# One step of a fused attention and mixing kernel: the low rank term's second product in one pass on stacked strips, and products of ones where the plan has TensorE wait

## The chip, the cores and the metric

The kernel runs on one core of a Trainium2 chip. The metric is the device time of one execution in microseconds (us), the median of several runs. TensorE (PE) multiplies into PSUM, VectorE (DVE) and ScalarE (ACT) empty PSUM and do the elementwise work, GpSimd (POOL) does elementwise work in SBUF, and SyncE (SP) issues most transfers, in order.

## What is computed

Three stages follow one another for a batch of 4, 576 positions and 512 features; the change touches the second line of the middle one.

```python
# 1. windowed attention, 8 heads of 64, window 128, with a linear bias
scores = where(mask, q @ k.T / 8 + bias, -1e9); x = softmax(scores) @ v      # (4, 576, 512)
# 2. low rank mixing over positions, then a two layer product
h = (x.transpose(0, 2, 1) @ U) @ V         # U is 576 x 32, V is 32 x 576
u = x + h.transpose(0, 2, 1)               # the low rank term is added to x
x = u + maximum(u @ w_ch1, 0) @ w_ch2      # 512 -> 2048 -> 512
# 3. gated mixing
a = maximum(x @ w_in, 0); g, v = a[..., :512], a[..., 512:]
v = (v - mean(v)) / sqrt(var(v) + 1e-6)
out = (g * (einsum('ts,bsd->btd', w_spatial, v) + b_spatial)) @ w_out
```

## The kernel before

All work is held in a list of tasks, each with an engine (or a choice of engines), a cost in planned microseconds, and the buffers that it reads and writes. `Plan.run` schedules the list eight times (`forward`, and `latest` for new priorities), takes the plan that ends first, and emits the instructions of the tasks in that order. Each engine then works its own instructions strictly in the emitted order. A task may sit on ACT or DVE (`copy` with two engines) or on POOL or DVE, as the plan finds better. The costs in the list are the planner's alone; what an instruction takes is seen in the trace.

The attention of a batch goes through four pairs of heads (`heads`): scores on TensorE (L1044), the bias and maximum on DVE (L1055), the exponential on ACT (L1060), the division on DVE or POOL (L1082, L1080; in the first batch it is put off to L1135), transpositions on TensorE (L1090) with copies to SBUF (L416 on ACT, L417 on DVE), and the product with v (L1128). The result is `u`, one tile of 128 features by 576 positions for each pair of heads. `turned` transposes it (L1155). `low_rank` then works in two steps:

- `mix` (L1171) multiplies with U. The four pairs' results, 32 rows each, lie as four strips in one PSUM tile `t`; a copy takes them to `th` in SBUF (tile th, L416).
- `up` (L1184) multiplies each strip with the matching 32 rows of V, for 288 positions at a time, in float32. The four pairs use four strips of rows of the array at once. DVE adds each product to `u` (L1189).

In the first batch `low_rank` is called twice, for pairs 0 and 1 and for pairs 2 and 3; in the other three once for all pairs. Float32 products show as two records each in the trace, products in float32r as one. Elsewhere the kernel gets float32's accuracy from float32r by splitting an operand into a high part (rounded) and a low part (the rest), with three products.

The low rank weights come early: V arrives as raw 64 bit words (raw), is put together on ACT and DVE into `v4` (L452 to L465, tile v), and four transfers (L983) spread it to `v32`.

When `u` of a batch is complete, ACT and POOL split it (L529, L532) and TensorE begins a group of the two layer product for 512 positions (`early_group`: L545 to L547, evacuated by L551 and L552; then L584 to L586, added by L594). Three such groups are worked among the attention of later batches. Their weights are put together on DVE (L458 to L465, tile st), too. The last low rank term is worked at 184 us; after it TensorE goes on through the two layer product and the gated stage until the end. `turn_over` (L991) is a task of before: nine float32 products of ones (tile hot) at the very beginning.

## Time and profile before

| | us |
|---|---|
| median of three runs (714.07 to 714.25) | 714.19 |
| the profiled execution | 713.79 |
| its span, from the first to the last instruction | 712.0 |

The profiled execution has 1.79 us outside its span, and it lies 0.40 us under the median. Busy time counts an engine's instructions from start to modelled end; matmuls overlap, so that a start to start distance says more than a duration. "Idle before" is the time in which the engine had nothing in hand, with what ended it.

### The profile page before, as it was taken

The page shows a single profiled execution, that of the slowest core. Times are in us where ns is not written, and L with a number is a line of the kernel's source. Part 1 is how long each engine was busy: PE and PEld are TensorE (multiplying, and loading weights), DVE is VectorE, ACT ScalarE, POOL GpSimd, SP SyncE. Part 2 cuts the span into 40 slices and gives each one's busy share as a digit, 9 for nine tenths or more (in the row PEclk, how much of TensorE's full clock was granted, in tenths as well). Part 3 has the DMA queues.
Part 4 walks back from the last instruction along what each step waited for, and adds up shares of the span by engine and source line. Part 5 has one row for each costly group of instructions (what it writes and reads, how often), then busy time and mean ns, then how long its engine had stood idle before and what let it go on. Part 6 is the DMA issues. An engine that isn't in the chain of part 4 may idle for free.

```text
span 712.0 us, 14829 instructions
## 1 busy us (share of the span) xinstructions
PE 701.7 (99%) x5434; PEld 637.8 (90%) x5434; DVE 576.0 (81%) x1637; ACT 394.0 (55%) x1082; POOL 75.0 (11%) x114
## 2 busy tenths in 40 slices
PE   8989999999999999999999999999999999999998
PEld 6767778778799999999999999999998898898896
DVE  6999996775597999999695998696589989859561
ACT  7878666564353655547253562544267566566352
POOL 2243330310400000000000000040010100100000
DMA  8865212210074166628475555447694202100102
GB/s 233 280 221 161 66 52 82 72 53 2 1 225 157 42 228 220 223 106 267 149 225 175 168 195 185 144 148 264 239 386 174 80 30 68 54 22 0 60 1 75
DMA packets 58799, 98.48 MB, mean 138 GB/s; under 512 B 8357, under 2 KB 38309, under 8 KB 58726
## 3 DMA queue, kind: packets, MB, share of 16 engines
q1 hardware_dynamic: 58437, 97.23, 41.2%
q8 instruction: 43, 0.70, 0.4%
q14 instruction: 31, 0.25, 0.1%
q10 hardware_dynamic: 288, 0.30, 0.1%
HBM read 67.67 MB, written 29.54 MB: 137 GB/s over the span
## 4 chain that ended last, share of the span: by engine, by line
PE 88%; DVE 7%; ACT 2%; DMA 1%; issue 1%; POOL 0%; SPq 0%; POOLq 0%; ACTq 0%
PE sc L586 8%; PE sc L584 8%; PE sc L585 8%; PE at L885 6%; PE at L886 6%; PE at L887 6%; PE at L1128 3%; PE sc L1044 2%; PE sc L1423 2%; PE sc L1421 2%; PE sc L1422 2%; PE at L1090 2%; PE at L1423 2%; PE at L1421 2%; PE at L1422 2%; PE acc L584 2%
## 5 line engine op out<-in xcount | busy, mean ns | idle before, releaser
L584 PE MATMUL sc<-h,wa 128*128 128x384 f32 (+1 forms) x328 | 110.6, 337 | 0.0
L585 PE MATMUL sc<-h,wa 128*128 128x384 f32 (+1 forms) x328 | 110.5, 337 | 0.0
L586 PE MATMUL sc<-hl,wa 128*128 128x384 f32 x320 | 108.7, 340 | 0.0
L1060 ACT ACTIVATE p<-p,nmax 128x192 f32<-128x192 f32 (+2 forms) x144 | 61.5, 431 | 10.2 <-DVE nmax L1055 10.0
L584 PEld LDWEIGHTS sc<-h,wa 128*128 128x128 f32 x328 | 61.6, 188 | 0.3
L585 PEld LDWEIGHTS sc<-h,wa 128*128 128x128 f32 x328 | 61.5, 187 | 0.3
L933 DVE TENSOR_TENSOR y<-sc,y 128x384 f32<-128x384 f32 (+1 forms) x96 | 40.7, 450 | 25.6 <-PE sc L586 25.3
L885 PE MATMUL at<-xd,wa 128*128 128x384 f32 x180 | 60.9, 338 | 0.0
L886 PE MATMUL at<-xd,wa 128*128 128x384 f32 x180 | 60.8, 338 | 0.0
L887 PE MATMUL at<-xd,wa 128*128 128x384 f32 x180 | 60.8, 338 | 0.0
L586 PEld LDWEIGHTS sc<-hl,wa 128*128 128x128 f32 x320 | 60.1, 188 | 0.0
L1055 DVE CUSTOM_DVE_ANT_0 p<-sc,bias 128x192 f32<-128x192 f32 (+2 forms) x144 | 40.3, 328 | 12.7 <-PE sc L1044 12.4
L905 ACT COPY c<-at 128x384 f32<-128x384 f32 x54 | 25.8, 478 | 39.2 <-PE at L887 38.9
L416 ACT CAST wa<-st 128x256 fp32r<-128x256 f32 (+1 forms) x62 | 28.1, 475 | 25.2 <-DVE st L465 13.1
L897 ACT ACTIVATE h<-c 128x384 fp32r<-128x384 f32 x54 | 28.4, 526 | 19.7 <-DVE c L892 19.5
L892 DVE TENSOR_TENSOR c<-at,c 128x384 f32<-128x384 f32 x54 | 29.8, 551 | 8.2 <-PE at L887 4.9
L885 PEld LDWEIGHTS at<-xd,wa 128*128 128x128 f32 x180 | 33.8, 188 | 0.0
L886 PEld LDWEIGHTS at<-xd,wa 128*128 128x128 f32 x180 | 33.8, 188 | 0.0
L887 PEld LDWEIGHTS at<-xd,wa 128*128 128x128 f32 x180 | 33.8, 188 | 0.0
L1044 PE MATMUL sc<-kr,qr 64*64 64x192 f32 (+2 forms) x576 | 31.7, 319 | 1.2 <-DMA qr<-in_qT 0.7
L1090 PE MATMUL at<-ident,p 128*128 128x128 f32 x208 | 31.1, 281 | 1.5 <-DVE p L1082 1.4
L1090 PEld LDWEIGHTS at<-ident,p 128*128 128x128 f32 x208 | 23.0, 140 | 10.4 <-issue 3.3
(407 smaller groups left out, 2007.7 us busy)
## 6 DMA issues: line engine op xcount, KB each, us to landing
wa<-in_w SPq DMA_DIRECT2D x32, 512.0 KB, 4.3
xd<-formsa SPq DMA_DIRECT2D x24, 192.0 KB, 3.0
qr<-in_qT SPq DMA_DIRECT2D x15, 288.0 KB, 3.3
kr<-in_kT SPq DMA_DIRECT2D x15, 288.0 KB, 4.0
vr<-in_v SPq DMA_DIRECT2D x16, 256.0 KB, 4.3
raw<-in_w_in SPq DMA_DIRECT2D x8, 512.0 KB, 3.9
kepts<-raw SPq DMA_DIRECT2D x14, 288.0 KB, 2.1
out<-h SPq DMA_DIRECT2D x15, 256.0 KB, 2.0
```

Source lines behind the costliest of these rows:

```text
L584: nc.tensor.matmul(o, wt[:, 0, 0, c], hh[:, j], start=i == 0 and x == 0, stop=False, skip_group_check=True)
L585: nc.tensor.matmul(o, wt[:, 1, 0, c], hh[:, j], start=False, stop=False, skip_group_check=True)
L586: nc.tensor.matmul(o, wt[:, 0, 0, c], hl[:, j], start=False, stop=i == len(wts) - 1, skip_group_check=True)
L885: nc.tensor.matmul(o.ap(), wh()[:, k], xh.ap(), start=start and k == 0, stop=False, skip_group_check=True)
L886: nc.tensor.matmul(o.ap(), wl()[:, k], xh.ap(), start=False, stop=False, skip_group_check=True)
L887: nc.tensor.matmul(o.ap(), wh()[:, k], xl.ap(), start=False, stop=k == 1, skip_group_check=True)
L892: P.add("DVE", dve(N3), lambda: nc.vector.tensor_tensor(out=out.ap(), in0=ps_.ap(), in1=sb.ap(), op=ALU.add), r=[ps_, sb], w=[out], prio=0)
L933: P.add("DVE", dve(m), lambda acc=acc, dst=dst, s=s, m=m, o=o: nc.vector.tensor_tensor(out=dst[:, s : s + m], in0=acc[:, 0, o : o + m], in ...
L1044: nc.tensor.matmul(s[o : o + 64, c0 : c0 + k1 - k0], qr[d, 64 * t : 64 * t + 64], kr[d, k0:k1], start=True, stop=True, skip_group_check=True)
L1055: nc.vector.tensor_tensor_reduce(out=o(), in0=s[:, c0 : c0 + nk], in1=bias_t[:, pair, t % 2, 192 - nk :], scale=-0.125, scalar=BIG, op0=AL ...
L1060: nc.scalar.activation(out=o(), in_=o(), func=AF.Exp, scale=-1.0, bias=nmax[:, sl, t : t + 1], accum_out=sums[:, sl, t : t + 1])
L1090: P.add("PE", 0.109, lambda pt=pt, n_=n_, s0=s0: nc.tensor.transpose(pt[:, n_ - s0], p[:, n_ * 128 : n_ * 128 + 128], ident), r=[p.part(t) ...
```

## The change

`up` no longer takes one strip of 32 rows per product. For each pair the strip of `t` is split into a high and a low part, and three strips are laid into `four`, a tile with 128 rows for each pair (the fourth strip stays zero): the high part once, the low part once, and the high part once more. `v32` now holds the high part of V in its first 64 rows and the low part in the other 64, so that one float32r product over all 128 rows is the sum of three partial products. Each pair's strips take three small instructions: a copy on ACT or DVE, a difference on DVE, and the second copy on ACT or DVE. They are planned at 0.27 us on ACT and 0.3 on DVE, longer than the planner's formula gives a copy of all four strips at once. Every product is a task of its own, with its own PSUM tile. V's split costs a copy on ACT and a difference on DVE ahead of the four transfers.

The other part is `fill`: a task on TensorE may carry a float32 product of ones into the tile that it is about to write. `Plan.run` emits up to three of them ahead of a task that the plan starts before 90 us, one for each 0.25 us that the plan leaves TensorE without work before it. The tasks that carry one are the scores, the transpositions, the spreading of the divisors (L1101), the product with v, `mix`, the new products and the first layer of the early groups.

```diff
@@ -138,10 +138,11 @@
 class Task:
-    __slots__ = ("eng", "cost", "emit", "ways", "prio", "deps", "succ", "left", "before", "start", "lat", "port", "mode")
+    __slots__ = ("eng", "cost", "emit", "ways", "prio", "deps", "succ", "left", "before", "start", "lat", "port", "mode", "fill")
...
 PASSES = 8
+FILL = 0.25, 3, 90.0
@@ -156,12 +157,12 @@
-    def either(self, ways, r=(), w=(), prio=0, lat=0.0, deps=(), port=False, mode=None):
+    def either(self, ways, r=(), w=(), prio=0, lat=0.0, deps=(), port=False, mode=None, fill=None):
...
         t = Task()
-        t.ways, t.prio, t.lat, t.port, t.mode = {way[0]: way for way in ways}, prio, lat, port, mode
+        t.ways, t.prio, t.lat, t.port, t.mode, t.fill = {way[0]: way for way in ways}, prio, lat, port, mode, fill
         d = set(deps)
@@ -220,7 +221,12 @@
             self.latest()
+        end = 0.0
         for t, t.eng, t.cost, t.emit, t.start in min(plans)[2]:
+            if t.eng == "PE":
+                for _ in range(min(FILL[1], int((t.start - end) / FILL[0])) if t.fill and t.start < FILL[2] else 0):
+                    t.fill()
+                end = t.start + t.cost
             t.emit()
@@ -552,6 +558,10 @@
+    def ones_into(o):
+
+        return lambda: nc.tensor.matmul(o(), hot.ap(), hot.ap(), start=True, stop=True, skip_group_check=True)
+
     def early_group(t0, n, wts, prio, evac, spare):
@@ -562,7 +572,8 @@
                 P.add("PE", 12 * mm(n), lambda f1=f1, j=j, wt=wt: first_of(f1[:, j], wt, hs, ls),
-                      r=[p for x in hs + ls for p in x[2]] + [wt.part(0), wt.part(1)], w=[f1], prio=prio)
+                      r=[p for x in hs + ls for p in x[2]] + [wt.part(0), wt.part(1)], w=[f1], prio=prio,
+                      fill=ones_into(lambda f1=f1, j=j: f1[:, j, :128]))
             hh, hl = r_h.new([128, w, n], F32R), r_h.new([128, w, n], F32R)
@@ -965,24 +976,27 @@
                   w=[p.part("zero")], prio=-1)
-    r_xt, r_th = Ring(in_att, "xt", 2), Ring(in_att, "th", 2)
+    r_xt, four = Ring(in_att, "xt", 2), constant("four", [128, 4, 128], F32R)
+    P.add("POOL", 0.3, lambda: nc.gpsimd.memset(f32(four.ap()), 0.0), w=[four.part(pair) for pair in range(4)], prio=-1)
...
     u32 = constant("u32", [128, 5, RANK], F32)
-    v32 = constant("v32", [128, S], F32)
+    v32 = constant("v32", [128, S], F32R)
...
         n = S // 2
-        v4 = constant("v4", [128, 1, n], F32)
+        v4, v4h = constant("v4", [128, 1, n], F32), Ring(in_left, "y", 0, more=["y_4"]).new([128, n], F32R)
         single(v4, [(0, block(V, 0, RANK, i // 2 * n, i // 2 * n + n), slice(RANK * i, RANK * i + RANK)) for i in range(4)],
                1, n, prio_v, None, early_v)
+        P.add("ACT", act(n, 0.09), lambda: nc.scalar.copy(out=v4h.ap(), in_=v4[:, 0]), r=[v4], w=[v4h], prio=K["vc"])
+        minus(("DVE",), n, lambda: v4[:, 0].bitcast(F32R), lambda: v4[:, 0], lambda: f32(v4h.ap()), r=[v4h], w=[v4], prio=K["vc"])
         for q in range(2):
-            for d in range(2):
-                P.dma(64, n, lambda q=q, d=d: nc.sync.dma_start(
-                    out=v32[64 * d : 64 * d + 64, q * n : q * n + n], in_=v4[64 * q : 64 * q + 64, 0]),
-                    r=[v4], w=[v32.part((q, d))], prio=K["vc"])
+            for d, (src, t) in enumerate(((lambda: f32(v4h.ap()), v4h), (lambda: v4[:, 0], v4))):
+                P.dma(64, n, lambda q=q, d=d, src=src: nc.sync.dma_start(
+                    out=f32(v32[64 * d : 64 * d + 64, q * n : q * n + n]), in_=src()[64 * q : 64 * q + 64]),
+                    r=[t], w=[v32.part((q, d))], prio=K["vc"])
@@ -1045,7 +1059,8 @@
             scored = [P.add("PE", 4 * max(sum(64 * min(t + 1, 3) for _, t, _ in tiles if t % 2 == o) for o in range(2)) / 2400 + 0.1,
-                  score, r=[x.part(c) for x in (qr, kr) for c in CUTS if c < 64 * tiles[-1][1] + 64], w=list(s.values()), deps=filled, prio=p0 + 1, mode="quarters")]
+                  score, r=[x.part(c) for x in (qr, kr) for c in CUTS if c < 64 * tiles[-1][1] + 64], w=list(s.values()), deps=filled, prio=p0 + 1, mode="quarters",
+                  fill=ones_into(lambda s=next(iter(s.values())): s[:, :128]))]
             for _, t, _ in tiles:
@@ -1088,7 +1103,7 @@
                     P.add("PE", 0.109, lambda pt=pt, n_=n_, s0=s0: nc.tensor.transpose(
-                        pt[:, n_ - s0], p[:, n_ * 128 : n_ * 128 + 128], ident), r=[p.part(t) for t in ts] + [p.part("zero")], w=[pt], prio=p0 + 5)
+                        pt[:, n_ - s0], p[:, n_ * 128 : n_ * 128 + 128], ident), r=[p.part(t) for t in ts] + [p.part("zero")], w=[pt], prio=p0 + 5, fill=ones_into(lambda pt=pt, n_=n_, s0=s0: pt[:, n_ - s0]))
                 copy(engines("e", "ACT"), 128 * (s1 - s0), lambda s0=s0, s1=s1: x[:, s0:s1], pt.ap, PSUM, r=[pt], w=[x.part(g)], prio=p0 + 6)
@@ -1101,7 +1116,7 @@
-                P.add("PE", 320 * 4 / 2400 + 0.1, spread, r=[dg, ones], w=rs, prio=p0 + 4.5, mode="quarters")
+                P.add("PE", 320 * 4 / 2400 + 0.1, spread, r=[dg, ones], w=rs, prio=p0 + 4.5, mode="quarters", fill=ones_into(lambda: rs[0][:, :2]))
                 r = r_d.new([128, 9, D], F32)
@@ -1129,7 +1144,8 @@
-            P.add("PE", 13 * 64 * 4 / 2400 + 0.2, pv, r=[vr, last] + [x.part(g) for g in range(4)], w=os_, prio=p0 + 8, mode="quarters")
+            P.add("PE", 13 * 64 * 4 / 2400 + 0.2, pv, r=[vr, last] + [x.part(g) for g in range(4)], w=os_, prio=p0 + 8, mode="quarters",
+                  fill=ones_into(lambda: os_[0][:, :2]))
             if plain:
@@ -1154,7 +1170,7 @@
                         x[:, c - c0, i], ub[:, TOK[c][0] : TOK[c][0] + 128], ident),
-                        r=[ub.part(0), ub.part(1)], w=[x], prio=p0 + 8.5)
+                        r=[ub.part(0), ub.part(1)], w=[x], prio=p0 + 8.5, fill=ones_into(lambda x=x, c=c, c0=c0, i=i: x[:, c - c0, i]))
             copy(engines("h", "ACT"), 256 * len(cs), lambda c0=c0, cs=cs: xt[:, c0 : c0 + len(cs)], x.ap, PSUM,
@@ -1162,8 +1178,7 @@
         sc, tp = (r_sc0, r_at0) if b == 0 else (r_sc, r_at)
-        rows = slice(pairs[0] * 32, pairs[-1] * 32 + 32)
-        t, th = tp.new([128, 128], F32), r_th.new([128, 128], F32)
+        t = tp.new([128, 128], F32)
@@ -1172,20 +1187,23 @@
         P.add("PE", 5 * 4 * 128 / 2400 + 0.1, mix, r=[u32] + [xts[h].part(c) for h in {p // 2 for p in pairs} for c in (0, 2, 4)],
-              w=[t], prio=p0, mode="quarters")
-        copy(engines("t", "ACT"), 128, lambda: th[rows], lambda: t[rows], PSUM, r=[t], w=[th], prio=p0 + 0.05)
+              w=[t], prio=p0, mode="quarters", fill=ones_into(t.ap))
+        strip = lambda g: slice(32 * g, 32 * g + 32)
+        for pair in pairs:
+            part, low = four.part(pair), 0 if pair == 1 else 1
+            high = lambda to, pair=pair, **kw: P.either([
+                ("ACT", 0.27, lambda: nc.scalar.copy(out=four[strip(to), pair], in_=t[strip(pair)])),
+                ("DVE", 0.3, lambda: nc.vector.tensor_copy(out=four[strip(to), pair], in_=t[strip(pair)]))], r=[t], w=[part], prio=p0 + 0.05, **kw)
+            high(pair)
+            P.add("DVE", 0.3, lambda pair=pair, low=low: nc.vector.tensor_tensor(
+                out=four[strip(low), pair], in0=t[strip(pair)], in1=f32(four[strip(pair), pair]), op=ALU.subtract), r=[t], w=[part], prio=p0 + 0.05)
+            high(2 if pair < 2 else 0, lat=0.3)
         for s0 in (0, 288):
             sl = slice(s0, s0 + 288)
-            outs = [(sc, tp)[pair % 2].new([128, 288], F32) for pair in pairs]
-
-            def up(sl=sl, outs=outs):
-                for pair, o in zip(pairs, outs):
-                    d = slice(pair * 32, pair * 32 + 32)
-                    nc.tensor.matmul(o.ap(), th[d], v32[d, sl], start=True, stop=True)
-
-            P.add("PE", 4 * 288 / 2400 + 0.1, up, r=[th] + list(v32.parts.values()), w=outs, prio=p0 + 0.1, mode="quarter rows")
-            for pair, o in zip(pairs, outs):
-                ub = u[b][pair]
+            for pair in pairs:
+                o, ub = (sc, tp)[pair % 2].new([128, 288], F32), u[b][pair]
+                P.add("PE", mm(288), lambda pair=pair, o=o, sl=sl: nc.tensor.matmul(o.ap(), four[:, pair], v32[:, sl], start=True, stop=True),
+                      r=[four.part(pair)] + list(v32.parts.values()), w=[o], prio=p0 + 0.1, fill=ones_into(lambda o=o: o[:, :128]))
                 P.add("DVE", dve(288), lambda o=o, ub=ub, sl=sl: nc.vector.tensor_tensor(
```

## Rows read from the trace of the kernel before

**Rows 1.** The page: busy time of the engines, share of the span, instructions

```profile
PE 701.7 (99%) x5434; PEld 637.8 (90%) x5434; DVE 576.0 (81%) x1637; ACT 394.0 (55%) x1082; POOL 75.0 (11%) x114
```

**Rows 2.** Busy time by stretch: stretch, length, engines (instructions), granted clock, DMA

```profile
0.00:20.00 20.00, 17.70 (x296) 13.71 (x296) 12.68 (x70) 15.21 (x63) 4.08 (x17) 1.00 0.81 235
20.00:40.00 20.00, 18.93 (x320) 13.85 (x313) 18.90 (x76) 16.60 (x58) 6.67 (x6) 1.00 0.94 304
40.00:60.00 20.00, 17.80 (x224) 12.70 (x218) 20.00 (x74) 14.55 (x51) 7.05 (x9) 1.00 0.48 154
60.00:80.00 20.00, 19.55 (x253) 15.48 (x248) 20.00 (x71) 17.24 (x56) 10.13 (x15) 1.00 0.44 129
80.00:100.00 20.00, 19.98 (x290) 14.70 (x294) 18.80 (x64) 11.95 (x41) 5.65 (x6) 1.00 0.20 62
```

**Rows 3.** The chain that ended last, by line: 0 to 80 us, then 80 to 190

```profile
by line: DVE p L1055 12.1%; DVE p L1082 11.1%; ACT p L1060 10.6%; DMA qr<-in_qT 8.6%; DVE ph L417 6.4%; DVE st L465 5.3%; PE at L1128 4.6%; DVE st L462 4.6%; issue 4.6%; POOL x L532 3.3%; PE sc L1044 3.2%; DVE st L458 3.1%; DVE h L552 3.0%;
...
by line: PE at L1128 14.8%; PE at L1090 11.8%; PE sc L1044 11.6%; PE acc L584 10.2%; PE acc L586 7.6%; PE acc L585 7.6%; PE f L545 6.9%; PE f L547 6.7%; PE f L546 6.6%; PE at L1155 5.6%; PE sc L1184 3.7%; PE at L1171 3.4%; PE sc L585 1.0%; 
```

**Rows 4.** TensorE in order of time, second batch: start, length, line, records

```profile
88.39 0.40 PE L585 MATMUL acc<-h,wa 128*128 128x512 f32 x1
88.63 0.39 PE L586 MATMUL acc<-h,wa 128*128 128x512 f32 x1
88.94 0.51 PE L1184 MATMUL sc<-v,th 32*128 32x288 f32 x1
...
89.64 0.50 PE L584 MATMUL acc<-h,wa 128*128 128x512 f32 x1
89.98 0.40 PE L585 MATMUL acc<-h,wa 128*128 128x512 f32 x1
```

**Rows 5.** TensorE in order of time, first batch, pairs 0 and 1

```profile
30.50 0.51 PE L1184 MATMUL sc<-v,th 32*128 32x288 f32 x1
...
31.67 0.87 PE L1090 MATMUL at<-ident,p 128*128 128x128 f32 x6
```

**Rows 6.** TensorE in order of time, gated stage: float32r products of 288 columns

```profile
545.18 0.30 PE L1574 MATMUL acc<-wf,x 128*128 128x288 f32 x1
...
545.97 0.29 PE L1577 MATMUL acc<-we,ve 128*128 128x288 f32 x1
```

**Rows 7.** TensorE in order of time, start: the products of ones

```profile
1.04 2.50 PE L991 MATMUL f<-hot 128*128 128x128 f32 x10 [1.04 <-DVE hot L950]
...
4.38 1.16 PE L991 MATMUL f<-hot 128*128 128x128 f32 x8
```

**Rows 8.** Instructions by line or tile: count, shortest, median, longest in ns, starts

```profile
L416 ACT COPY th<-at x5: 260/266/267, 29.1 to 180.9; 128x128 f32<-128x128 f32 x3, 64x128 f32<-64x128 f32 x2
L1189 DVE TENSOR_TENSOR u<-at,u x16: 434/448/453, 31.4 to 185.4; 128x288 f32<-128x288 f32 x16
L602 DVE TENSOR_TENSOR fg<-y,fg x32: 205/215/226, 510.5 to 696.5; 128x64 fp32r<-128x64 f32 x32
```

**Rows 9.** DVE in order of time, from 20 and from 39 us

```profile
20.32 0.82 DVE L1135 TENSOR_TENSOR u<-at,y 128x320 f32<-128x320 f32 x2 [0.49 <-PE at L1128]
...
39.64 3.06 DVE L1082 TENSOR_SCALAR p<-p,rinv 128x192 f32<-128x192 f32 x9
...
42.96 0.45 DVE L1189 TENSOR_TENSOR u<-sc,u 128x288 f32<-128x288 f32 x1
43.32 0.44 DVE L1189 TENSOR_TENSOR u<-at,u 128x288 f32<-128x288 f32 x1
```

**Rows 10.** ACT in order of time, 39 to 46 us

```profile
41.95 0.48 ACT L416 COPY ph<-at 128x384 f32<-128x384 f32 x1 [1.42 <-PE at L1090]
43.60 0.48 ACT L416 COPY ph<-at 128x384 f32<-128x384 f32 x1 [1.17 <-PE at L1090]
```

**Rows 11.** SyncE in order of time, 19 to 24 us: start, length, transfer

```profile
19.86 1.18 SPq L983 DMA_DIRECT2D v<-v  x2
21.14 0.52 SPq L1008 DMA_DIRECT2D qr<-in_qT  x1
```

## The prediction

> **What bounds the kernel now.** I read the page first: TensorE is busy for 701.7 us, 99% of the span [rows 1]. Busy time flatters matmuls, so the second view is the busy time by stretch, where the reader should compare TensorE with DVE: in the first 80 us TensorE has waits of 2.30, 1.07, 2.20 and 0.45 us, 6.0 in all, while DVE is at 18.90 of 20 from 20 us on and at 20.00 of 20 from 40 to 80; from 80 on TensorE is at 19.98 of 20 [rows 2]. The third view, the chain that ended last, says the same by cause. Up to 80 us its largest pieces are DVE's and ACT's (bias and maximum 12.1%, division 11.1, exponential 10.6), and of TensorE's lines only two show among them, 4.6 and 3.2%; from 80 to 190 all the lines shown are TensorE's, the low rank product (L1184) with 3.7% [rows 3]. So the kernel has two rules. Before 80 us a microsecond counts if it lies on DVE (or on ACT, where the chain runs over it); after that each microsecond of TensorE's work counts whole. The change touches both stretches.
>
> **Part 1, TensorE's work in the second to fourth batch: a gain.** A float32 block of four pairs stands between two products of an early group. From the start of the product before it, 88.63, to the second start behind it, 89.98, are 1.35 us. Without the block these would be two starts of 0.24 (88.39 to 88.63), 0.48; the block with its changes of the array's form costs 0.87 [rows 4]. There are six such blocks after 80 us, two per batch: 5.2 us. The new form needs 24 float32r products of 128 rows by 288 columns. The gated stage runs that shape: six starts from 545.18 to 545.97, 0.132 each [rows 6]. 24 of them are 3.2 us. Gain: 2.0 us, all of it where TensorE sets the time.
>
> On this step a rule of the Trainium skill speaks against the change. "TensorE: Matmul & The Clock Gate", section "Why this matters for your kernels", says that products over 32 rows placed in four strips run at once, and gives 3.07 times for four of them, a single one of 32 rows taking as long as one of 128. If the six blocks' 5.2 us became 3.07 times as long, the sum would be 10.8 us worse in place of 2.0 better. The rows decide otherwise: the strips are float32 and the full rows float32r, and 0.132 is measured.
>
> **Part 2, the same in the first batch: little.** Two calls, each with two blocks back to back: 30.50 to 31.67, 1.17 us [rows 5], against four products, 0.53. That is 1.3 us less in two calls, but in the stretch where TensorE waits anyway. TensorE's two visible lines hold 7.8% of the chain there [rows 3], so I book 0.1 of it; the bounds are 0 and 1.3.
>
> **Part 3, the strips: a loss before 80 us.** One ACT copy of all strips took 0.266 us [rows 8]; a batch now has twelve small instructions. The first batch adds four differences on DVE and eight copies, each on ACT or DVE. The trace has no DVE instruction of this shape. The nearest are the addition from PSUM over 288 columns, 448 ns long but started every 0.36 us (42.96, 43.32), and one over 64 columns, 215 ns [rows 8, 9]. Taking 160 columns off the first, at the 233 ns per 224 columns between the two, gives 0.36 - 0.17 = 0.19, say 0.2 us of DVE each. Four are 0.8 us. Two of them fall near 30 us, where DVE still has 1.10 us free in 20 [rows 2], and I count half; the other two fall behind the nine divisions from 39.64, where it has none [rows 9]. That is 0.6 on the path. The bounds: nothing, if the plan moves as much of DVE's choice work to ACT or POOL; 0.8 if no wait covers them, and 2.4 if all eight copies went to DVE as well. I take the low side for the copies, since ACT waits 1.42 and 1.17 us just there [rows 10]. If that cover were gone, each would cost its 0.2.
>
> In the later batches the twelve stand at 87 us and after, beside TensorE's own work of the early groups: between `mix` and the first block TensorE has two sets of three such products to do already. DVE is at 18.80 of 20 from 80 to 100 [rows 2], so the four differences of the second batch, 0.8 us, fit into what is left; I book nothing, and 0.8 if that slack is taken.
>
> **Part 4, V's split: nothing.** One copy on ACT, one difference of 288 columns on DVE at 0.36 to 0.45 [rows 8, 9], once. DVE waits 0.49 us at 20.32, right behind V's last step [rows 9]. The four transfers (L983) issue at 19.86 and after [rows 11] and would go some 0.9 us later (copy, difference, two handovers); behind them in SyncE's queue stands the load of q for a later pair at 21.14 [rows 11]. First to need `v32` is the product at 30.50 [rows 5], so seven us of slack hide it. Without it V's split would cost 0.4 of DVE. The clearing of `four` on POOL is at the start, on an engine busy for 75.0 us in all [rows 1].
>
> **Part 5, products of ones: nothing, or a loss.** Eight records of the present ones take 1.16 us less the last one's overlap [rows 7]; two records make a product, so one costs some 0.25 on TensorE. The plan places them where it expects a wait, and TensorE has 6.0 us of waits before 80 [rows 2]. If plan and chip wait at the same places the products are hidden there. If not, each one behind which real work is ready puts 0.25 on TensorE, which before 80 us is mostly off the chain. They give nothing that the rows show: ten records took 2.50 us at the start, then eight took 1.16 [rows 7]; that is the step from 1.2 to 2.4 GHz, after the products of ones and the first scores. The starts of 0.24 and 0.132 later on [rows 4, 6] are those of the high level, and the granted clock is 1.00 in every stretch [rows 2]. There is no lower level left in this kernel to lift. Price: 0, at most 0.25 for each.
>
> **The sum.** -2.0 (part 1) - 0.1 (part 2) + 0.6 (part 3) + 0 + 0 = -1.5 us. From the profiled execution's 713.79 that is 712.3; the median lies 0.40 higher, so 712.7 us, just past the 0.2% (1.4 us) that a measurement of this kernel tells from no change.
>
> **Rivals.**
> *TensorE's whole saving arrives.* If the plan finds room for the strips on ACT and POOL, and the early part moves up by all of part 2, it is -2.0 - 1.3 = -3.3: 710.9 us. For it: TensorE is busy for 99% of the span [rows 1]. Against it: DVE's 20.00 of 20 [rows 2].
> *The strips eat the gain.* 0.8 in the first batch, 0.8 in the second, 0.4 for V, each without cover: +2.0 against -2.0, 714.2 us. For it: DVE leads the chain for 80 us [rows 3].
> *Products of ones in the way.* Between 10 and 60 us they stand ahead of scores and transpositions whose results DVE waits for. At 0.25 each it takes six that delay the chain to undo -1.5, and twelve to be slower by 0.2%; fifteen give 716.4. For it: one plan's gaps need not be the chip's. Against it: before 80 us the chain is seldom on TensorE.
> *The clock falls.* TensorE waits longer for strips in the first batch, and works at the low level after it: twice the 0.13 or 0.24 us per start. Work of four us at the high level would take four more: 716.7. The waits of before, 6.0 us in 80, brought no fall [rows 2]. The same Trainium skill page, section "Part 1: The HAM clock gate", has the clock fall after idling; on its side a row of this trace shows only the low level of the beginning.
> *The new products don't follow one another at 0.132.* Alone among other work each costs its whole 0.30 us [rows 6]: 24 are 7.2 us, 2.0 worse than the blocks in place of 2.0 better, 716.7 us. The rule of part 1 points that way; the rows of the gated stage do not.
>
> **Chances.** Forecast 0.42, of which 0.34 past the 0.2% and 0.08 short of it; whole saving 0.13; strips 0.23; products of ones 0.17; clock 0.03; starts 0.02. Faster 0.47, same 0.31, slower 0.22. The plan is also drawn up anew, which can shift waits among the 6.0 us either way. The range reaches from the whole saving, 710.9, to 715.8, twelve products of ones too many; the forecast's own range is 711.6 to 713.6.
>
> **What would show it.** Right: 32 one-record products of 128 rows by 288 columns at some 0.13 per start in place of 64 records; TensorE's waits before 80 us no more than 0.6 us longer in sum beside the ones; DVE's part of the chain ending by 81 us. Wrong: DVE's part of the chain reaching a us or more beyond 81 (strips), products of ones with the next record starting right behind them and no wait ahead (ones in the way), or starts of 0.2 us for transpositions after 5 us (clock).

## The result

The changed kernel takes 722.37 us (median of four runs, 722.06 to 723.35) against 714.22 of the kernel before beside it (714.07 to 715.04): a ratio of 1.0115, 95% interval 1.0101 to 1.0129. It is slower by 8 us; the prediction was 712.7 in 710.9 to 715.8. The span of the profiled execution went from 712.0 to 720.5 us.

Which stretch lost the time? All of it lies ahead of the gated stage's first 384-column product on TensorE: it starts at 191.9 us before and at 200.3 after, and behind it both run 520 us. In the page, TensorE's busy time and count, against [rows 1]:

```profile
PE 707.7 (98%) x5456; PEld 646.5 (90%) x5456; DVE 580.4 (81%) x1657; ACT 400.8 (56%) x1101; POOL 76.8 (11%) x121
```

The busy time by stretch, with the columns of [rows 2]:

```profile
40.00:60.00 20.00, 16.33 (x204) 12.55 (x205) 18.17 (x56) 10.51 (x32) 8.26 (x8) 1.00 0.52 175
60.00:80.00 20.00, 18.98 (x213) 14.77 (x213) 18.70 (x71) 17.44 (x57) 9.43 (x13) 1.00 0.46 135
```

From 40 to 80 us DVE, which stood at 20.00 of 20 twice [rows 2], now has waits of 1.83 and 1.30 us, and ACT has fallen from 14.55 to 10.51 in 40 to 60: the engines wait for one another. The chain that ended last, up to 80 us, no longer runs over DVE and ACT first, as in [rows 3], but over TensorE:

```profile
by line: PE sc L1058 14.1%; PE at L1143 11.1%; PE at L1105 8.9%; DVE p L1097 7.4%; ACT p L1075 4.8%; PE f L1005 4.5%; DVE p L1070 3.7%; PE sc L563 3.3%; PE at L1171 3.1%; DVE st L471 2.9%; PE at L1116 2.7%; DVE ph L423 2.3%; DVE st L468 2.3
```

L1058, L1143 and L1105 are scores, values and transpositions, work that was there before; L563 are the products of ones, on the chain with 3.3%.

The 24 products after 80 us are there as foreseen, one record each. TensorE in order of time, second batch, where the prediction expected six blocks of 0.87 us to become products of 0.132:

```profile
97.02 0.39 PE L597 MATMUL acc<-h,wa 128*128 128x512 f32 x1
97.24 0.42 PE L1205 MATMUL sc<-v,four 128*128 128x288 f32 x2
97.53 0.40 PE L1205 MATMUL at<-v,four 128*128 128x288 f32 x1
97.85 0.40 PE L1205 MATMUL sc<-v,four 128*128 128x288 f32 x1
98.14 0.53 PE L1205 MATMUL at<-v,four 128*128 128x288 f32 x2
99.37 0.50 PE L595 MATMUL acc<-h,wa 128*128 128x512 f32 x1 [0.69 <-DVE y L605]
```

They don't follow at 0.13: there are 0.32 and 0.29 us between the starts at 97.53, 97.85 and 98.14, and behind them TensorE waits 0.69 us for `y` at L605, a DVE step of other work. DVE in the same stretch says why, and ACT beside it:

```profile
95.70 0.88 DVE L1198 TENSOR_TENSOR four<-at,four 32x128 fp32r<-32x128 f32 x3
96.89 0.29 DVE L1198 TENSOR_TENSOR four<-at,four 32x128 fp32r<-32x128 f32 x1 [0.32 <-ACT four L1195]
97.51 0.29 DVE L1196 CAST four<-at 32x128 fp32r<-32x128 f32 x1 [0.32 <-ACT four L1195]
97.83 0.43 DVE L613 TENSOR_TENSOR st<-st 128x256 f32<-128x256 f32 x1
98.17 0.42 DVE L613 TENSOR_TENSOR wa<-st,wa 128x256 fp32r<-128x256 f32 x1
98.62 0.69 DVE L605 TENSOR_TENSOR y<-acc,u 128x512 f32<-128x512 f32 x1
```

```profile
96.61 0.26 ACT L1195 CAST four<-at 32x128 fp32r<-32x128 f32 x1 [0.21 <-DVE four L1198]
97.22 0.26 ACT L1195 CAST four<-at 32x128 fp32r<-32x128 f32 x1 [0.36 <-DVE four L1198]
```

L1195, L1196 and L1198 are the strips: copy on ACT, copy on DVE, difference. They are twelve steps from 94.49 to 98.09, 3.6 us. Three differences follow one another on DVE (95.70); eight of the others start only when the step before them on the other engine has ended, with waits of 0.21 to 0.36 us. Two further steps of DVE (L613) and the addition that empties the accumulator (L605, at 98.62) stand behind them in DVE's order, and TensorE's next product needs that accumulator.

### The profile page after: what moved, and what is told of

Its sections match the earlier page's. It is cut to its first block, busy times and chain, and to the rows that moved or that the text cites. A ratio compares the mean times of both kernels' runs of the same rounds, so it can differ in the third digit from the quotient of the medians.

```text
span 720.5 us, 14917 instructions
## 1 busy us (share of the span) xinstructions
PE 707.7 (98%) x5456; PEld 646.5 (90%) x5456; DVE 580.4 (81%) x1657; ACT 400.8 (56%) x1101; POOL 76.8 (11%) x121
## 4 chain that ended last, share of the span: by engine, by line
PE 92%; DVE 5%; ACT 2%; issue 0%; POOL 0%
PE sc L597 8%; PE sc L595 8%; PE sc L596 8%; PE at L896 6%; PE at L897 6%; PE at L898 6%; PE at L1143 4%; PE sc L1058 3%; PE at L1105 3%; PE sc L1441 2%; PE sc L1439 2%; PE sc L1440 2%; PE at L1439 2%; PE at L1441 2%; PE at L1440 2%; PE f L551 1%
## 5 line engine op out<-in xcount | busy, mean ns | idle before, releaser
L1105 PE MATMUL at<-ident,p 128*128 128x128 f32 x208 | 30.7, 279 | 1.4 <-DVE p L1097 1.0
L1058 PE MATMUL sc<-kr,qr 64*64 64x192 f32 (+2 forms) x576 | 31.9, 318 | 0.0
L1520 ACT CAST x<-h 128x256 fp32r<-128x256 f32 x56 | 22.0, 407 | 17.9 <-DVE h L1483 13.3
```

Of the source, the lines that this page charges most:

```text
L1058: nc.tensor.matmul(s[o : o + 64, c0 : c0 + k1 - k0], qr[d, 64 * t : 64 * t + 64], kr[d, k0:k1], start=True, stop=True, skip_group_check=True)
L1105: P.add("PE", 0.109, lambda pt=pt, n_=n_, s0=s0: nc.tensor.transpose(pt[:, n_ - s0], p[:, n_ * 128 : n_ * 128 + 128], ident), r=[p.part(t) ...
```

## The experiments

"This" is the median; the ratio is to the kernel before on the same chip, whose median was between 713.97 and 714.39 in every group of runs; the clock is the mean granted one of the profiled execution.

```
                                          this     ratio, interval           clock
the change                                722.37   1.0115 [1.0101, 1.0129]   1.000
no products of ones             (e1)      720.92   1.0092 [1.0075, 1.0108]   0.995
ones in the kernel before       (e2)      716.11   1.0020 [1.0010, 1.0029]   1.000
at most one of ones a wait      (e3)      721.90   1.0107 [1.0092, 1.0122]   0.999
e1, strips planned short        (e4)      719.83   1.0084 [1.0064, 1.0104]   0.991
before, plan drawn anew         (e5)      715.41   1.0018 [1.0009, 1.0028]   1.000
before, products planned singly (e6)      725.56   1.0156 [1.0141, 1.0172]   0.995
e1, first strip of a pair alone (e7)      714.17   0.9998 [0.9989, 1.0008]   1.000
e1, 16 planning passes          (e8)      716.44   1.0031 [1.0019, 1.0044]   0.998
e1, a tile for each pair        (e9)      722.62   1.0098 [1.0077, 1.0120]   0.998
e9 with all products of ones    (e10)     722.17   1.0100 [1.0083, 1.0117]   1.000
e9, 16 passes                   (e11)     716.20   1.0029 [1.0018, 1.0040]   0.998
e9, ones from 36 to 60 us       (e12)     720.79   1.0081 [1.0066, 1.0096]   1.000
e9, second copy from the first  (e13)     717.89   1.0053 [1.0033, 1.0072]   0.995
e13, 16 passes                  (e14)     715.29   1.0012 [1.0003, 1.0022]   0.997
e13, ones from 36 to 60 us      (e15)     718.29   1.0055 [1.0038, 1.0072]   1.000
e13, chain told to the planner  (e16)     719.98   1.0079 [1.0064, 1.0094]   0.995
two readings, no stacking       (e17)     716.47   1.0035 [1.0022, 1.0048]   0.995
e17, 16 passes                  (e18)     715.87   1.0028 [1.0013, 1.0043]   0.998
```

The change, e1, e7, e9, e12, e13 and e15 have the same order on every engine, up to what is left out or put in, so the same TensorE instruction can be looked up in each. That gives the ladder on which most of what follows rests (starts in us, from the timelines; what each is late against e7 behind the sign):

```
TensorE instruction                      e7       change        e1            e12           e15
first transposition                       6.84     7.95 +1.1     7.67 +0.8     7.48 +0.6     7.83 +1.0
mix of pairs 0 and 1, first batch        28.17    29.67 +1.5    28.98 +0.8    28.79 +0.6    29.16 +1.0
mix of pairs 2 and 3                     40.00    43.12 +3.1    40.90 +0.9    41.37 +1.4    41.86 +1.9
their first new product                  42.64    47.12 +4.5    45.54 +2.9    45.35 +2.7    45.44 +2.8
scores of the next pair                  45.12    50.61 +5.5    48.16 +3.0    48.84 +3.7    48.69 +3.6
first product of the early groups        48.61    54.09 +5.5    54.41 +5.8    52.33 +3.7    52.17 +3.6
before the second batch's products       91.23    97.02 +5.8    96.62 +5.4    95.23 +4.0    95.03 +3.8
behind six of them                       92.40    99.37 +7.0    98.96 +6.6    97.58 +5.2    96.75 +4.4
before the third batch's                137.21   144.18 +7.0   143.77 +6.6   142.39 +5.2   141.54 +4.3
behind six of them                      138.54   146.84 +8.3   146.43 +7.9   145.06 +6.5   143.98 +5.4
before the fourth batch's               183.34   191.62 +8.3   191.22 +7.9   189.85 +6.5   188.78 +5.4
behind                                  183.97   192.79 +8.8   192.39 +8.4   191.03 +7.1   189.41 +5.4
first 384-column product                190.77   200.30 +9.5   199.88 +9.1   198.53 +7.7   196.51 +5.7
```

Each column is one profiled execution. e7's is its fastest (713.04 us) and e1's its slowest (722.16), so the two are 9.1 us apart here and 6.75 in the medians. 0.6 to 1.5 us of the lateness is there before any strip. Part of it differs between executions: the last four products of ones of the start (L1005) take 1.25 us in e7 and 2.07 in e1. In the change three more products of ones also stand ahead of the first scores, which start at 4.76 and not at 3.48. After that the lateness grows at the strips: by 2.0 us in e1 at pairs 2 and 3 of the first batch, and by 1.2, 1.3 and 1.2 us in the later batches. It also grows at the products of ones (the change, e12 and e15, between 36 and 50 us). In e1 it grows by 2.8 us between the scores at 48.16 and the early groups, where there is no strip; that is the clock, below. In between it nearly stands still.

**The products of ones (e1, e2, e3).**

```diff
-FILL = 0.25, 3, 90.0
+FILL = 0.25, 0, 90.0      # e1; e3: 0.25, 1, 90.0
```

e2 puts FILL and the `fill=` of each TensorE step into the kernel before, whose order it keeps: 18 products.

> The changed kernel with none of the 27 products of ones between its tasks; the order of all other instructions is the same. If the ones stand behind TensorE's waits and not in them, each costs about its 0.27 us of TensorE (7.28 us of starts for 54 records) and the time falls by some 7 us, to 715 to 716 us. If they are hidden in the waits and the strips with the new order made the loss, the time stays at 721 to 723 us.

> The kernel before with its own low rank term and its own order, and only the products of ones added: the plan places 18 of them. If a product of ones costs its full time, 714.2 + 18 x 0.27 = 719 us. If they are hidden in the waits, 714 us, within 0.2%.

> The changed kernel with at most one product of ones ahead of a task in place of three: 14 in place of 27, all else in the same order. If each costs its time, 722.4 - 13 x 0.27 = 718.9 us, half way to the kernel without any. If only the first of each group delays something, the time stays near 722; if the waits hide the first and the second and third are too many, it falls to 715 to 716.

Without the 27 products (54 records) the time falls by only 1.45 us (722.37 to 720.92), where 7 were expected if each cost its time. With e3's fewer ones it falls by 0.5, inside the spread of its executions. 18 of them put 1.7 us into the kernel before (716.11 against 714.39 on its chip). That is less than their full time, 18 times 0.27, and more than nothing. They are a loss, and not the main one. How they cost is in the rows. A product of ones writes the PSUM tile of the instruction it stands before, and so becomes free with it, not ahead of it. The change, TensorE at the scores of the last pair of the first batch, and DVE waiting for them:

```profile
49.74 0.94 PE L563 MATMUL sc<-hot 128*128 128x128 f32 x6 [0.55 <-DVE u L1207]
50.61 1.10 PE L1058 MATMUL sc<-kr,qr 64*64 64x64 f32 x24
```

```profile
51.64 0.22 DVE L1070 CUSTOM_DVE_ANT_0 p<-sc,bias 128x64 f32<-128x64 f32 x1 [0.94 <-PE sc L1058]
```

The first row had waited 0.55 us for the additions into `u`, as the scores behind it would have; then three products of ones (six records) run, 0.87 us until the scores start, and DVE's first maximum ends a wait of 0.94. Nothing was filled there: the wait was over.

But they do one thing that the prediction ruled out. e1, busy time in 40 to 50 and 50 to 60 us, the sixth figure behind the stretch being the granted clock, and TensorE:

```profile
40.00:50.00 10.00, 6.17 (x61) 4.37 (x61) 8.66 (x20) 4.60 (x11) 4.95 (x6) 0.87 0.51 176
50.00:60.00 10.00, 9.49 (x118) 7.33 (x117) 8.24 (x34) 5.42 (x21) 2.91 (x4) 0.79 0.43 127
```

```profile
45.54 0.53 PE L1205 MATMUL at<-v,four 128*128 128x288 f32 x2 [1.75 <-ACT four L1195]
...
48.16 1.98 PE L1058 MATMUL sc<-kr,qr 64*64 64x64 f32 x24 [0.48 <-DVE u L1207]
50.08 3.02 PE L1143 MATMUL at<-ph,vr 128*64 128x64 f32 x60
```

TensorE waits 1.75 us for a strip at 45.54, 0.35 and 0.48 for additions behind it; then the 24 records of scores take 1.98 us and the 60 of values 3.02. In e7 the same take 1.10 and 1.76:

```profile
45.12 1.10 PE L1058 MATMUL sc<-kr,qr 64*64 64x64 f32 x24 [0.55 <-DVE u L1206]
46.16 1.76 PE L1143 MATMUL at<-ph,vr 128*64 128x64 f32 x60
```

That is the clock's lower level, 1.2 in place of 2.4 GHz; the granted clock is 0.87 and 0.79 there, and 1.00 with the products of ones. On the ladder e1 is 2.5 us ahead of the change at the scores and 0.3 behind it at the early groups: what the ones cost, the clock gives back. By the Trainium skill ("TensorE: Matmul & The Clock Gate", section "Part 1: The HAM clock gate") the clock falls after TensorE has idled; e1's trace agrees, with these rows.

**Which part of the strips (e7), and is it the order (e4, e5, e6, e8).** e7 keeps e1's order and makes the difference and the second copy of each pair emit nothing. It leaves out the low part of the first factor and one of the high part's two products: with V's low part for pairs 0 and 1, with V's high part for pairs 2 and 3, whose first copy lies beside V's low part. So e7 is a measure of time alone.

```diff
-            P.add("DVE", 0.3, lambda pair=pair, low=low: nc.vector.tensor_tensor(
-                out=four[strip(low), pair], in0=t[strip(pair)], ...
-            high(2 if pair < 2 else 0, lat=0.3)
+            P.add("DVE", 0.3, lambda: None, r=[t], w=[part], prio=p0 + 0.05)
+            P.either([("ACT", 0.27, lambda: None), ("DVE", 0.3, lambda: None)], ...)
```

> The changed kernel without products of ones and in the same order of all instructions, with two of each pair's three strip instructions left out (the difference and the second copy; the low rank term then lacks its low parts). If the strips' own time and the chain through them make the loss, the time falls from 720.9 by 3 us or more; if the order does, by less than 1.5 us (32 instructions of 0.2 to 0.3 us, of which eight to sixteen stand before 95 us).

714.17, the time of the kernel before: the 32 instructions that are left out cost 6.75 us (720.92 less 714.17) in e1's order, with all that follows from them; in e1 the fall of the clock is a part of it. That the products are planned singly, as in e7 too, is not the cause in this order. The busy time of the 32 is 0.26 to 0.30 us each, on two engines. The new products meet no wait for a strip in the second batch of e7, on TensorE:

```profile
91.23 0.39 PE L597 MATMUL acc<-h,wa 128*128 128x512 f32 x1
91.45 0.42 PE L1204 MATMUL sc<-v,four 128*128 128x288 f32 x2
91.72 0.29 PE L1204 MATMUL at<-v,four 128*128 128x288 f32 x1
91.85 0.30 PE L1204 MATMUL sc<-v,four 128*128 128x288 f32 x1
91.98 0.43 PE L1204 MATMUL at<-v,four 128*128 128x288 f32 x2
92.40 0.50 PE L595 MATMUL acc<-h,wa 128*128 128x512 f32 x1
92.73 0.40 PE L596 MATMUL acc<-h,wa 128*128 128x512 f32 x1
```

```profile
89.94 0.42 DVE L613 TENSOR_TENSOR st<-st 128x256 f32<-128x256 f32 x1
90.28 0.42 DVE L613 TENSOR_TENSOR wa<-st,wa 128x256 fp32r<-128x256 f32 x1
91.65 0.69 DVE L605 TENSOR_TENSOR y<-acc,u 128x512 f32<-128x512 f32 x1 [0.95 <-PE acc L597]
```

Here the starts are 0.13 to 0.14 apart, DVE's L613 ran at 89.94, and L605 waits for TensorE (0.95). TensorE's next product starts at 92.40, just behind L605's end at 92.34.

e4 plans the strips at the planner's standard cost for 128 columns instead of 0.27 and 0.3; e5 changes only the planned cost of the copy of `th` in the kernel before; e6 leaves that cost as it was and plans that kernel's float32 products one by one, as the change does its own; e8 gives the planner 16 passes. All four have other orders.

> The changed kernel with no products of ones and the strip steps planned by the formula for 128 columns (0.17 us on ACT, 0.2 on DVE) in place of 0.27 and 0.3, so that the order is drawn up anew. If longer planned steps are worth something, this is slower than the changed kernel without ones, by up to 2 us; if the planned cost does not matter, the two agree within 0.2%.

> The kernel before with one planned number changed: the copy of the low rank strips is planned at 0.27 us on ACT or 0.3 on DVE, where it was 0.17 and 0.2. No instruction is added or taken away; the plan comes out in another order. If a new order alone is worth several us (the order of before being a lucky one), the time rises by 2 to 6 us, to 716 to 720; if orders of one list are worth the same, it stays within 0.2% of 714.4.

> The kernel before with its float32 strips, but each product a task of its own, as in the changed kernel: 32 tasks in place of 10, no strips to split, V not split. If the finer tasks and the order that follows from them make the loss, 717 to 721 us; if the strips do, 714 to 715.

> The changed kernel without products of ones, planned in 16 passes in place of 8, so that the same instructions come in another order that the planner holds to be no longer. If the order decides, the time moves by more than 1.5 us from 720.9, either way; if the strips decide, it stays within 0.2%.

A plan drawn anew costs 1.3 us by itself in e5 (715.41 against 714.09), and the passes move the changed kernel by 4.5 (e1 to e8): the order is a lottery of this size, but no order tried brings the strips below the kernel before. So the 6.75 us are the strips' price in e1's order. In e8's order, where the whole kernel is 2.4 us above the kernel before, no run leaves the strips out. e4's 1.1 us are not separated from e1's interval. e6 tells one thing more: with the old products planned singly, and the order that follows, the kernel before takes 11.5 us longer, more than the 721 of its expectation. Its clock falls too (0.89 in 40 to 60 us, 0.94 in 60 to 80), and the shares of the two aren't separated.

**Through what do the strips cost (e9 to e16)?** The first theory was the tile: all four pairs' operands are quarters of one tile.

```diff
-    ..., constant("four", [128, 4, 128], F32R)
+    ..., [constant(f"four{i}", [128, 128], F32R) for i in range(4)]      # and four[pair] throughout
```

> The changed kernel without its products of ones, and each pair's stacked operand in a tile of its own instead of a quarter of one tile for all four; every engine's order is that of the run without the products (720.92 us, first 384-column product at 199.9 us). Theory A: the price of the strips is above all the chain across pairs, ACT waiting for DVE and DVE for ACT on the one tile, about 0.3 us at each turn, and its late start of the new products; with own tiles ACT's and DVE's strips run side by side, the first batch's new products start within about 1 us of the transposes instead of 1.9 us late, the 384-column product falls to 193-196 us, and the time is 714.5 to 717. Rival B: the strips cost by their number and their busy time, the waits only show it; then 719.5 to 721.5. Rival C: the high part's copy and the difference in one pair, ACT to DVE and back, is the chain that counts, which own tiles leave; then about half comes back, 717 to 719.

> The changed kernel with all its 27 products of ones, and own tiles for the pairs. Theory A: as the changed kernel minus what the own tiles give, 715.5 to 718.5, and above the same kernel without the products by about 1 to 2 us, since less waiting is left for them to fill. Rival: the products hold the clock at its upper level where it fell without them (0.87 and 0.79 at 40 to 60 us), and with the strips' chain gone that is worth more than their starts: then it is at or below the kernel without them.

> Own tiles, no products of ones, and 16 passes of the planner instead of 8, which gives the other order that ran in 716.44 us with the one tile. Theory A: the chain across pairs costs in this order too, and the time falls by 1.5 to 4 us, to 712.5 to 715, perhaps below the kernel before. Rival B (strips cost by number): 716 to 717. Rival C: this order was faster because it already lets the chain run beside other work; then 715.5 to 716.5.

> Own tiles, and of the products of ones only those planned between 36 and 60 us, 12 products, where the clock fell without any. If the clock is what these buy: granted clock 1.00 at 40 to 60 us and a time at or up to 1 us below the run with own tiles and no products. If their starts are all that they bring: above it by about 0.7 us (12 products at two starts of 0.13 us each, and their waits for the tiles that they write, less what stands idle).

Theory A fell: 722.62 (719.76 to 723.05) and 716.20 are no better than e1's 720.92 and e8's 716.44, and the strips still alternate. e10, at 722.17, is no faster than the change either. e9, ACT and DVE in the second batch:

```profile
93.78 0.25 ACT L1195 CAST four<-at 32x128 fp32r<-32x128 f32 x1 [0.21 <-DVE four L1198]
94.39 0.26 ACT L1195 CAST four<-at 32x128 fp32r<-32x128 f32 x1 [0.36 <-DVE four L1198]
```

```profile
94.06 0.29 DVE L1198 TENSOR_TENSOR four<-at,four 32x128 fp32r<-32x128 f32 x1 [0.32 <-ACT four L1195]
94.68 0.28 DVE L1196 CAST four<-at 32x128 fp32r<-32x128 f32 x1 [0.32 <-ACT four L1195]
```

Each of these steps waits for the step before it on the other engine, whichever pair that was for. With own tiles for the operands, what steps of different pairs still share is the mixed tile `t` in PSUM, which all of them read. So two readings of one PSUM tile by ACT and DVE seem to be put one after the other, and the planner, which has them run beside each other, doesn't know it. The next runs try that. "PSUM — Partial Sum Buffer" of the Trainium skill, section "PSUM bank collisions raise a hardware error", has two engines collide in one bank where they touch the same 32 partitions, readings included, and not where the partitions are others. The strips of two pairs lie in different ones, so by that page they might run at once; no run here shows it, since in each of these runs steps of different pairs wait for one another.

e13 takes the second copy of each pair from the first, in SBUF, and so cuts four of twelve readings, at the same number of steps and the same order:

```diff
-            high(2 if pair < 2 else 0, lat=0.3)                   # from t[strip(pair)]
+            high(2 if pair < 2 else 0, lambda pair=pair: four[pair][strip(pair)], lat=0.3)
```

e16 tells the planner that the eight readings follow one another (`deps=` from each to the next).

> Own tiles, no products of ones, and the second copy of each high part reads the first copy in SBUF instead of the mixed tile in PSUM; every engine's order is that of the run with own tiles (722.62 us). The waits in that kernel's program and trace follow the mixed tile: each strip step waits for the step before it that reads the same PSUM tile on the other engine, whichever pair it is for. Theory D: this chain over the one PSUM tile is the strips' price; eight of twelve readings stay, the differences then follow back to back on DVE and the second copies run beside them on ACT, so the stretch from the mix to the last strip falls from about 3.7 to 2.6 us in each of the later three batches and by 0.6 to 1 us in the two stretches of the first: 717 to 720. Rival B (number and busy time of the strips): 721 to 723. Rival E (DVE's and ACT's queues, strips ahead of other work, not the chain): 720.5 to 722.

> The same as the run before it, planned with 16 passes, in the order that took 716.2 us with own tiles. Theory D: 1 to 2.5 us less, 713.7 to 715.2. Rivals B and E: 715.5 to 716.5.

> Second copies from the first, and the 12 products of ones planned between 36 and 60 us, which took the run with own tiles from 722.62 to 720.79 us. If the clock is what they buy, clock 1.00 at 40 to 60 us and 1 to 2 us below the run with second copies from the first and no products; if that kernel waits less and its clock does not fall, no gain or up to 0.7 us above it.

> Second copies from the first, no products, and the planner is told that the eight readings of the mixed tile come one after another (a dependence from each to the next), so it books the true end of the strips; the order on the engines is another throughout. Theory D with a plan that misjudged the chain: the new products are set where their operand is ready, the first 384-column product comes at 192 to 195 us, 713 to 716. If the plan's belief does not matter, within 1 us of the run with second copies from the first, apart from the 1 us or so by which another order alone moved the kernel before.

717.89 against 722.62, in one order, and inside theory D's 717 to 720. Part of these 4.7 us is the clock: e9's executions were granted 0.993 to 0.998 in the mean, e13's 0.995 to 1.00. The cleanest pair is e12 and e15, both at clock 1.00: 720.79 (720.56 to 721.03) and 718.29 (718.06 to 718.80), 2.5 us for four readings of twelve. e15, second batch:

```profile
93.73 1.22 DVE L1198 TENSOR_TENSOR four<-at,four 32x128 fp32r<-32x128 f32 x4
94.97 0.21 DVE L1196 CAST four<-four 32x128 fp32r<-32x128 f32 x1
95.21 0.42 DVE L613 TENSOR_TENSOR st<-st 128x256 f32<-128x256 f32 x1
```

```profile
94.45 0.94 ACT L1195 CAST four<-four 32x128 fp32r<-32x128 f32 x3
```

Four differences in one run, three copies on ACT meanwhile, and no wait between: the strips end 2.9 us after they began, not 3.6, and L613 starts at 95.21. TensorE's wait for L605 falls from 0.69 to 0.53 us, and the new products before it lose theirs. On the ladder e15 gains 0.6, 0.2 and 1.0 us on e12 in the three later batches, 1.8 in sum. In the first batch it gains 0.5 more, once the 0.6 and 1.0 of the start are taken off; but its divisions there also meet GpSimd more luckily, by 1.0 us (last section). In e9 and e13, whose divisions go alike, the way from the mix of pairs 2 and 3 to their first new product is 0.5 us shorter (4.64 and 4.13). Of e15's 5.7 us behind e7 on the ladder, 1.0 is there at the start, 2.8 come before the second batch's products, where its 14 products of ones are too, and 1.9 in the three later batches. In the other order four readings fewer give 0.9 (e11 to e14, 716.20 to 715.29), a little under the 1 us that theory D asked for at least. The planner's knowledge alone gave nothing: e16's order is 2.1 us slower than e13's, so this part of the expectation failed.

The products of ones again: from e10 to e12, 26 records fewer, -1.4 us; from e9 to e12, the 28 records (14 products, not the 12 of the expectation) that hold the clock at 1.00 in 40 to 60 us, -1.8, inside e9's own spread; e13 to e15, +0.4 inside both. Single executions tell more. e13's two at a granted clock of 1.00 took 716.87 and 717.20 us, its two at 0.995 and 0.997 took 719.49 and 718.57; e15's four, at 0.999 and 1.00, took 718.06 to 718.80. So in e15 the ones buy off the clock's fall and cost about as much: they bring nothing.

**Two readings (e17, e18).** The high parts of all pairs in one copy, the low parts in one difference, no stacking: three products of 32 rows for a pair, four pairs beside each other, V's high and low part in two tiles. The aim was to keep float32r and drop the strips.

```diff
+        copy(engines("t", "ACT"), 128, lambda: th[rows, 0], lambda: t[rows], PSUM, ...)
+        P.add("DVE", 0.3, lambda: nc.vector.tensor_tensor(out=th[rows, 1], in0=t[rows], in1=f32(th[rows, 0]), op=ALU.subtract), ...)
...
+                for k, (i, v) in enumerate(((0, v32), (0, v32l), (1, v32))):
+                    for pair, o in zip(pairs, outs):
+                        nc.tensor.matmul(o.ap(), th[d, i], v[d, sl], start=k == 0, stop=k == 2)
```

> The float32r idea with two readings of the mixed tile for a batch instead of eight or twelve: one copy of all strips as the high part (as the kernel before copied th) and one difference of all strips, no stacking; V's high and low parts lie in two tiles in all four strips, and each product is three float32r products of 32 rows, four pairs beside each other on TensorE, as the kernel before ran its float32 ones. No products of ones. The order is another one throughout. Theory D: from the mix to the operand's end falls from 2.8 to 3.7 us to about 0.6 us, TensorE waits for no strip, the first 384-column product comes at 190 to 193 us and the time is 712.5 to 715.5, by what the order brings. If the strips' number or their readings were not the cause, it stays at 717 or above. Against it: 96 float32r products at a quarter of the rows, which no trace here has shown; the 64 float32 records took 5.77 us, so 2.9 us to 8.6 us for the 96.

> The same, planned with 16 passes instead of 8. Theory D: within 1.5 us of the run before it, either way, so 711.5 to 716; with the strips' chain gone the two orders differ by less than the 4.5 us by which they differ in the changed kernel without the products of ones (720.92 and 716.44 us).

716.47 and 715.87: some 6 us better than the change, and still 2 us above the kernel before. e17 missed its range by 1.0 us, e18 kept to its own. The operand is ready 0.7 us after the mix and no strip chain is left, yet the gain isn't there. TensorE, second batch:

```profile
91.48 0.40 PE L597 MATMUL acc<-h,wa 128*128 128x512 f32 x1
91.81 0.40 PE L1203 MATMUL sc<-v,th 32*128 32x288 f32 x1
91.81 0.40 PE L1203 MATMUL at<-v,th 32*128 32x288 f32 x1
91.81 0.39 PE L1203 MATMUL sc<-v,th 32*128 32x288 f32 x1
91.82 0.40 PE L1203 MATMUL at<-v,th 32*128 32x288 f32 x1
92.05 0.29 PE L1203 MATMUL at<-v32l,th 32*128 32x288 f32 x1
92.05 0.29 PE L1203 MATMUL sc<-v32l,th 32*128 32x288 f32 x2
...
92.41 0.50 PE L595 MATMUL acc<-h,wa 128*128 128x512 f32 x1
92.75 0.39 PE L596 MATMUL acc<-h,wa 128*128 128x512 f32 x1
```

Counted as in [rows 4], to the second start behind, from 91.48 to 92.75 are 1.27 us; less two starts of 0.23 are 0.81 for a block, against 0.87. The blocks of the later batches that can be counted alike are about 0.1 us shorter, so six blocks give some 0.5 us. In the first batch the clock falls, 0.83 in 40 to 60 us, where TensorE waits for copy and difference. How much of the 2 us is the clock and how much the new order, no run separates. No version tried is faster than the kernel before.

## Why the prediction was wrong

**Part 3 failed, and with it the sign.** It booked 0.6 us for the strips, all of it in the first batch and nothing in the later ones, with 0.2 us of DVE for each difference and 2.4 as its upper bound. The 32 instructions cost 6.75 in the change's order. Where these lie is best seen on e9 and e7, the fastest execution of each (719.76 and 713.04), which are 0.05 us apart at the first mix: 2.1 us at the first batch's pairs 2 and 3, 0.6 where the clock falls, 3.8 in the later batches. Three things were missed.
- *The price of one.* No row of that shape was at hand, and a column count was scaled. A copy of a strip takes 0.26 us on ACT and 0.28 on DVE, differences in a row start 0.30 apart (four in 1.22 us, e15), and a successor on the other engine starts some 0.3 after its predecessor.
- *The chain.* I counted busy time on two engines and took ACT's waits of 1.42 and 1.17 us [rows 10] for cover. All readings of `t` follow one another: twelve are 3.6 us. Four readings fewer give 2.5 us back (e12 to e15), 1.8 of them in the later batches on the ladder.
- *Who stands behind it.* The prediction named no instruction queued behind the strips on DVE. In the later batches it is L605, and TensorE waits for it through the one accumulator: on the ladder +1.2, +1.3 and +1.2 us in the change, 3.7 in sum, where 0.8 was the worst that I allowed. That DVE was at 18.80 of 20 [rows 2] said nothing about the place. In the first batch they stand ahead of the additions into `u`, on which the next scores wait: from the mix of pairs 2 and 3 to those scores e7 takes 5.1 us, e1 7.3, the change 7.5. Of e1's 2.2 us more, 1.0 is the divisions of the last section.

How much of the rest of the 6.75 is the differences' own time on a full DVE, how much the eight readings that remain, and how much the divisions and the clock, the runs don't separate; taking away the first strip's readings as well was not tried.

**Part 1 was two thirds of what I took.** Counted as in [rows 4], e7's six products in a row in the second batch take 1.04 us (91.23 to 92.73 less two starts of 0.23), the other two 0.13 each: 1.3 against 1.74 for two blocks. In the third and fourth batch the eight take 1.45 and 1.06. That is 3.8 us in all, 1.4 less than the blocks' 5.2, where 2.0 was booked. What I left out is the accumulator. The products do follow one another at 0.13; but behind the six stands a product that needs the accumulator emptied by L605, which ends at 92.34, and in the third batch TensorE waits 0.15 us for it. In the change the same count (97.02 to 99.70), without the wait of 0.69, is 1.53 and 0.26: 1.8 us, no gain, because the products wait for strips.

In e17 four float32r products over 32 rows start at 91.81, 91.81, 91.81 and 91.82, and the next four 0.24 later. So the rule of the Trainium skill that I weighed against the change ("TensorE: Matmul & The Clock Gate", "Why this matters for your kernels": products over 32 rows in four strips run at once) holds in float32r as well. I had the traces' float32 strips alone. By the rows a block takes 0.87 us in float32, 0.81 in e17 and 0.63 on full rows (3.8 over six in e7), so full rows are the shortest form on TensorE, and their price lies on the other engines.

**Part 5: a small price, and a wrong reason for it.** 0 was booked with 0.25 each as a bound; 27 cost 1.45 net. Three of them alone put the first scores from 3.48 to 4.76. "There is no lower level left in this kernel to lift" held for the kernel before (granted clock 1.00 in its every stretch) and not for the changed one. The rival "products of ones in the way" was right about the mechanism (0.87 us at the last scores of the first batch, 1.7 us in e2) and not about the size of the whole. The rival "the clock falls" happens as it was described, after a wait for a strip, once the ones are gone.

**Parts 2 and 4** are not measured by themselves. e7 has the products, the first copies and V's split, and it is no faster than the kernel before although TensorE's products are 1.4 us shorter after 80 us; so no saving of the first batch shows, and what takes the 1.4 back stays open. The rival "the strips eat the gain" had the cause, at 2.0 us instead of 6.75. The range ended 6.6 us too low: its upper end was set by the ones (712.7 and twelve at 0.25 are 715.7, not 715.8), and the strips' bound left out that steps can wait for each other.

The sum as measured, in the change's order: e7 against before, no difference that can be measured (714.17 and 714.1); the 32 strip steps +6.75, with the clock's fall and the divisions that come with them; the products of ones +1.45; together 722.4. They are differences of medians, and hold for this order.

## What to carry to other kernels

When one instruction becomes several that read the same PSUM tile on two engines, price the chain from first to last, handover included, and ask what stands behind its last step in each engine's order; busy time and an engine's slack over 20 us don't show it. Filler work that writes the waiting instruction's own tile is released with it, so it delays it: it pays only by keeping the clock up, and only where it would fall. Two kernels in one order can be compared instruction by instruction, and a ladder of starts shows at which step time is lost; take off first what the two executions differ by before the changed step.

## What the runs showed of the hardware that was not expected

A division on DVE takes 0.31 us alone and over four times as long beside a GpSimd step. The change, first batch, DVE and POOL:

```profile
42.37 0.31 DVE L1097 TENSOR_SCALAR p<-p,rinv 128x192 f32<-128x192 f32 x1
```

```profile
42.76 1.33 DVE L1097 TENSOR_SCALAR p<-p,rinv 128x192 f32<-128x192 f32 x1
```

```profile
42.69 1.28 POOL L614 TENSOR_TENSOR wa<-st,wa 128x512 fp32r<-128x512 f32 x1 [0.33 <-ACT wa L422]
```

The 128x192 division at 42.37 takes 0.31, the one at 42.76 takes 1.33 and ends 0.1 us behind the POOL step of 1.28 us that started at 42.69. Which of the two starts first decides, by hundredths of a us. In e7 and e15 the division in this place starts 0.01 and 0.02 us ahead of that POOL step and takes 0.31 and 0.30; in the change, e1, e9, e10, e12 and e13 it starts 0.00 to 0.07 us behind it and takes 1.33 to 1.39. In e7 and e15 the next division is the long one, and no other. In the rest a second one comes to stand beside the next POOL step (L538, 44.42 in the change): six divisions took 3.75 us in the change and 3.79 in e1, where e7's took 2.74. That is one more us in the first batch, which no count of instructions shows. "SBUF — State Buffer" of the Trainium skill, section "Who interferes with whom", has only the port pair that DVE and GpSimd share cause contention, as an exclusive lock; these rows agree.
